# Joining f64 weights in a PSUM bank, reordering the first attention tiles, and splitting w_out one block later

## The chip, the cores and the metric

The kernel runs on one core of a Trainium2 chip. The metric is the device time of one execution in microseconds (us), the median of several runs. The engines are TensorE (PE; its weight loads are PEld), VectorE (DVE), ScalarE (ACT), GpSimd (POOL) and SyncE (SP), which here only issues transfers. Each works through its own queue in program order and waits on semaphores for the others.

## The reference

```
k_p, v_p = k, v averaged over groups of 8 positions      # 8 batches, 8 heads, 576 -> 72
attn = softmax(q @ k_p.T / 8) @ v_p                       # + 1e-9 in the denominator
x = attn as 4608 tokens x 512
h = x @ w_in                                              # 512 -> 2048, w_in and w_out arrive as f64
g = where(h >= 1, h, where(h <= -1, 0, (h + 1)**2 / 4))
y = g @ w_out                                             # 2048 -> 512
e = argmax(y @ w_gate) of 8 experts, p = its softmax weight
out = p * (max(y @ w1[e], 0) @ w2[e])
```

## The kernel before

The 4608 tokens are 36 tiles of 128 rows, in ten blocks of 3, 4 x 7, 3 and 2 tiles. The routed experts follow and are not touched by the change.

**A block of the feed-forward** runs over m = 0 to 15, the 128-wide slices of the hidden dimension. `f1(j, m)` forms h for the slice with 12 matmuls in ps0 or ps1; `f2(j, m)` adds the slice's part of y with 9 or 12 matmuls into ps2 and up. f1 runs two steps (`AHEAD`) ahead of f2. Each operand is split into a high part and a remainder (hi, lo), so a product takes three matmuls (L593 to L595, L621 to L623). Behind f1's matmuls come L600 (VectorE, clamp), L601 (ScalarE, square), then, put off through the list `later`, `larger`: L605 (VectorE, maximum) and L606 (ScalarE, high part of g), and at the next flush `lower`: L264 on VectorE (remainder of g), which frees ps0 or ps1. `slot(j, s)` is called twice per step, s = 2m and 2m + 1, here called the even and the odd half of a step. It calls `tick` (block 0 only), then one or two of the attention units of the next block's tiles, then `flush`, which runs what stands in `later`; in block 0 also one pooling step of the next batch's K and V.

**Converting the weights.** w_in and w_out are f64; slices are loaded as pairs of 32-bit words into six buffers RB, and 32 conversions (`order`) make f32 of them in block 0 and before it:
- a, `convert_a`: ScalarE copies the scaled high word into the target (L527; WOF for w_out, DFI for w_in, three or four buffers each) and the sign into SGN (L531);
- b, `convert_b`: two VectorE operations, the "pair": L539 joins low word and sign into CV, which is the PSUM bank ps5, and L542 shifts the target and joins CV into it. They are put on the list `pend` and issued by `mix()`, at the latest by the next tick's `mix(4)`;
- c, `convert_c`: ScalarE casts the high part (L549), POOL subtracts (`low_part`, L264), and for w_out SP stores both parts, 512 KB, to wo_d (L552).

`tick` number n does mix(4), the load of a later slice, c(n - 2), a(n) and b(n). Eight ticks are issued around the first two f1; in block 0's loop there is one in each half-step for m = 0 to 11, one in each of steps 12 and 13, and none after that. Conversions count from 0. From block 1 on `load_out` brings both parts of w_out back, 512 KB a step, on the ScalarE queue.

**Attention of a tile t** is cut into units: q transposed (TensorE; L368 copies), scores (TensorE L312; VectorE L319, L321 twice each; then exp, ScalarE L326, and the row sum L376, L378, L379), the probabilities turned (first three tiles: TensorE L412 and ScalarE L414, two copies; tiles 3 to 6: VectorE transposes L396, L398, and an exchange through DRAM, p_d, on SP's queue), and the product with V (TensorE L425; ScalarE L431 high part of x, VectorE L432 low part). The division is on POOL (L382, L390). Before block 0, K and V of batch 0 are pooled: K heads 0 to 3 on TensorE (`u_kp`), the others on VectorE (L249, one reduction) or POOL (L252 to L254), and tiles 0 to 2 are done with their units interleaved.

The order on each engine is the order in which these functions are called; nothing is reordered.

Of the kernel before, what the change touches and what calls it, by code (L numbers as in the profile page):

```python
# [8 lines left out]
F32 = mybir.dt.float32  # L9
# [15 lines left out]
def attention_ffn_routed_experts_kernel(  # L25
# [47 lines left out]
    wo_d = dram.tile([KF, 128, 2, DM], F32R, name="wo_d")  # L73
    yrow_d = dram.tile([NT + 128, ROW], F32, name="yrow_d")
# [35 lines left out]
    KB = [at(576 * i, 4 * SP_).rearrange("p (a c) -> p a c", a=4) for i in range(2)]  # L110
    QB = [at(1152 + 512 * i, 512) for i in range(2)]
    QB2 = at(6336, 512)
    QT = at(2176, 512)
    SC = [at(2688, 576), at(7616, 576)]
    HEAD = blocks[0][1]
    RAW = [at(3264 + 512 * i, 512, SP_) for i in range(3)]
# [7 lines left out]
    PZ = at(1152, 768).rearrange("p (a h j) -> p a h j", a=3, j=32)  # L124
# [162 lines left out]

    def u_kt_pair(b, c):

        pb = bank()  # L290
        nc.tensor.transpose(pb[:, 0:SP_], KP[:, c * 128:(c + 1) * 128], ident[0:SP_, 0:SP_])
        nc.scalar.activation(out=KB[b][:, c], in_=pb[:, 0:SP_], func=ACTF.Copy)

# [10 lines left out]
    def u_sc_all(t):  # L304
# [10 lines left out]
        sc, sc3, smx = sc_of(t), sc3_of(t), smx3[:, t % 3]  # L315
# [9 lines left out]
        def exps():  # L325
            nc.scalar.activation(out=sc, in_=sc, func=ACTF.Exp, scale=1.0 / 64)  # L326
            finish(t)
        if HEAD <= t < TURN0:
# [7 lines left out]
    SCH = at(6848, 576)  # L336
    PTX = [WOF[2][0:SP_], WOF[3][0:SP_], PT[:, 0], PT[:, 1]]
# [7 lines left out]
    def sc3_of(t):  # L345
        return sc_of(t).rearrange("p (h c) -> p h c", h=H)

    def pt_of(t, hf):
        return PTX[(2 * t + hf) % 4] if t < HEAD else PT[:, hf]
# [22 lines left out]
    def finish(t):  # L372
        sc3, ssm = sc3_of(t), ssm3[:, t % 3]

        def rest():
            nc.vector.tensor_reduce(out=ssm, in_=sc3, axis=AX.X, op=ALU.add)  # L376
            mix()
            nc.vector.tensor_scalar(ssm, ssm, 1e-9, None, op0=ALU.add)  # L378
# [144 lines left out]
    def convert_a(i):  # L523
        dst, rb = cvt_dst(i)

        high = rb[:, :, :, 1].bitcast(F32)
        nc.scalar.activation(out=dst.rearrange("p (a x) -> p a x", a=8), in_=high,  # L527
# [5 lines left out]
    def convert_b(i):  # L533
# [6 lines left out]
            out=ci, in0=rb[:, :, :, 0], scalar=29, in1=sg, op0=ALU.logical_shift_right,  # L540
            op1=ALU.bitwise_or))
        pend.append(lambda: nc.vector.scalar_tensor_tensor(  # L542
            out=di, in0=di, scalar=3, in1=ci, op0=ALU.logical_shift_left, op1=ALU.bitwise_or))

    def convert_c(i):
# [5 lines left out]
        if o:  # L551
            nc.sync.dma_start(out=r32(wo_d[m]), in_=r32(WO[:, m % 4]))  # L552
# [19 lines left out]
    def tick():  # L572
# [5 lines left out]
        for f, i in ((convert_c, n - 2), (convert_a, n), (convert_b, n)):  # L578
            if 0 <= i < len(order) and order[i]:
                f(i)  # L580
# [876 lines left out]
```

## Time and profile before

| what | value |
|---|---|
| median of 3 runs (lowest, highest) | 1401.77 us (1400.38, 1402.29) |
| the profiled execution's own time | 1404.79 us |
| its span, first to last instruction | 1402.8 us |
| granted TensorE clock, mean over the span | 0.993 |
| busy PE / DVE / ACT / POOL | 1357.5 / 778.1 / 433.7 / 358.7 us |
| busy in the first 38.10 us, PE / DVE / ACT / POOL | 23.60 / 22.32 / 18.67 / 19.50 us |
| one L326 / L431 on ScalarE | 0.69 / 0.58 us |
| one L601, 384 wide, on ScalarE | 0.62 us |
| one L379 on VectorE | 0.20 us |

The profile is one execution. A duration is given from the start of the work to its end, and on VectorE and ScalarE the next instruction often starts a little before the end of the one ahead. A busy TensorE is not one at its full rate. A note in square brackets on a timeline row is the engine's idle time before the instruction, and what ended it.

### The profile page before, as it was taken

The numbers are of one execution on the slowest core, as the hardware profiler recorded it, in microseconds if no ns is written. First come the engines' busy times: TensorE is split into PE (matmuls) and PEld (weight loads), VectorE is DVE, ScalarE is ACT, GpSimd is POOL, SyncE is SP. The second block draws the span as 40 slices with busy tenths as digits, with TensorE's granted clock in tenths as the row PEclk, the third lists the DMA queues.
The fourth block names the chain that finished last, engine by engine and source line by source line (L and its number), as shares of the span: only waits on it lengthen the run. The fifth ranks groups of instructions, "written<-read, shape, count | busy, mean of one in ns | idle before, by whom it ended". The sixth has DMA issues, their size and how long they took to land. (4 is left out here: it accounts for less than half of the span.)

```text
span 1402.8 us, 22101 instructions
## 1 busy us (share of the span) xinstructions
PE 1357.5 (97%) x8082; PEld 1112.8 (79%) x8082; DVE 778.1 (55%) x1577; ACT 433.7 (31%) x729; POOL 358.7 (26%) x520
## 2 busy tenths in 40 slices
PE   6878999999999999999999999999999999999998
PEld 4767778878878778788788888888878888888786
DVE  5798556565666666575666556455532333323426
ACT  4567332222222222223222223343111111111335
POOL 5384736004304203413310011022221211111212
PEclk9999999999999999999999999999999999999999
DMA  9786647436636555545553344572543223331235
GB/s 254 226 261 240 182 136 214 129 122 194 164 124 187 153 149 168 171 155 143 165 157 111 98 152 130 192 263 72 195 129 106 91 74 113 99 111 61 79 127 187
DMA packets 170701, 213.45 MB, mean 152 GB/s; under 512 B 83432, under 2 KB 114440, under 8 KB 170569
## 3 DMA queue, kind: packets, MB, share of 16 engines
q1 hardware_dynamic: 135992, 102.29, 25.2%
q10 hardware_dynamic: 26784, 88.16, 18.8%
q0 software_dynamic: 7792, 21.35, 4.8%
q8 instruction: 69, 1.13, 0.3%
q14 instruction: 64, 0.52, 0.1%
HBM read 188.30 MB, written 47.03 MB: 168 GB/s over the span
## 5 line engine op out<-in xcount | busy, mean ns | idle before, releaser
L593 PE MATMUL ps<-XT,W 128*128 128x512 f32 (+2 forms) x640 | 243.8, 381 | 6.8 <-DVE FG L264 3.0
L595 PE MATMUL ps<-XT,W 128*128 128x512 f32 (+2 forms) x640 | 237.9, 372 | 2.7 <-POOL W L264 2.7
L594 PE MATMUL ps<-XT,W 128*128 128x512 f32 (+2 forms) x640 | 238.1, 372 | 0.2 <-DVE XT L432 0.2
L621 PE MATMUL ps<-WO,FG 128*128 128x512 f32 x576 | 231.6, 402 | 1.3 <-ACT FX L601 1.1
L622 PE MATMUL ps<-WO,FG 128*128 128x512 f32 x576 | 225.9, 392 | 0.0
L623 PE MATMUL ps<-WO,FG 128*128 128x512 f32 x576 | 225.2, 391 | 0.0
L601 ACT ACTIVATE FX<-FX,half 128x512 f32<-128x512 f32 (+2 forms) x152 | 104.0, 684 | 386.0 <-DVE FX L600 348.2
L600 DVE TENSOR_SCALAR FX<-ps 128x512 f32<-128x512 f32 (+2 forms) x152 | 96.7, 636 | 117.7 <-PE ps L595 116.9
L593 PEld LDWEIGHTS ps<-XT,W 128*128 128x128 f32 x640 | 121.8, 190 | 32.1 <-issue 3.4
L719 POOL DMA_INDIRECT perm_d<-idt,POSI x36 | 35.2, 978 | 417.6 <-DVE SM L705 353.0
L993 DVE SCALAR_TENSOR_TENSOR FG<-ps,FG 128x512 fp32r<-128x512 f32 (+1 forms) x64 | 43.2, 675 | 175.4 <-ACT FG L992 172.9
L595 PEld LDWEIGHTS ps<-XT,W 128*128 128x128 f32 x640 | 121.7, 190 | 22.3 <-POOL W L264 4.0
L605 DVE TENSOR_TENSOR ps<-FX,ps 128x512 f32<-128x512 f32 (+2 forms) x152 | 97.5, 641 | 72.8 <-ACT FX L601 71.4
L594 PEld LDWEIGHTS ps<-XT,W 128*128 128x128 f32 x640 | 121.7, 190 | 17.8 <-DVE XT L432 0.5
L621 PEld LDWEIGHTS ps<-WO,FG 128*128 128x128 f32 x576 | 108.5, 188 | 26.4 <-issue 3.0
L623 PEld LDWEIGHTS ps<-WO,FG 128*128 128x128 f32 x576 | 108.6, 188 | 23.7
L606 ACT ACTIVATE FG<-ps 128x512 fp32r<-128x512 f32 (+2 forms) x160 | 88.8, 555 | 123.9 <-DVE ps L605 112.2
L264 DVE TENSOR_TENSOR FG<-ps,FG 128x512 fp32r<-128x512 f32 (+2 forms) x160 | 100.8, 630 | 44.3 <-ACT FG L606 40.6
L622 PEld LDWEIGHTS ps<-WO,FG 128*128 128x128 f32 x576 | 108.7, 189 | 19.8
L252 POOL TENSOR_TENSOR AT<-AT 72x256 f32<-72x256 f32 x106 | 81.2, 766 | 136.3 <-DMA AT<-in_v_dram 68.7
L992 ACT ACTIVATE FG<-ps 128x512 fp32r<-128x512 f32 (+1 forms) x64 | 37.4, 584 | 244.8 <-PE ps L989 231.2
L987 PE MATMUL ps<-XT,W 128*128 128x512 f32 (+1 forms) x256 | 98.9, 386 | 2.9 <-ACT XT L971 2.5
(230 smaller groups left out, 2176.0 us busy)
## 6 DMA issues: line engine op xcount, KB each, us to landing
WO<-wo_d ACTq DMA_DIRECT2D x144, 512.0 KB
AT<-in_moe_w_dram SPq DMA_DIRECT2D x30, 1024.0 KB
p_d<-AT SPq DMA_DIRECT2D x29, 384.0 KB
AT<-in_v_dram SPq DMA_DIRECT2D x59, 144.0 KB
wo_d<-WO SPq DMA_DIRECT2D x16, 512.0 KB
AT<-in_k_dram SPq DMA_DIRECT2D x56, 144.0 KB
PT<-p_d SPq DMA_DIRECT2D x58, 128.0 KB
yrow_d<-Y ACTq DMA_DIRECT2D x7, 1032.0 KB
```

Source lines behind the costliest of these rows:

```text
L264: eng.tensor_tensor(out=lo, in0=x, in1=r32(hi), op=ALU.subtract)
L593: nc.tensor.matmul(o, wi(m, 0, c), xh, start=(c == 0), stop=False)
L594: nc.tensor.matmul(o, wi(m, 0, c), xl, start=False, stop=False)
L595: nc.tensor.matmul(o, wi(m, 1, c), xh, start=False, stop=(c == KD - 1))
L600: nc.vector.tensor_scalar(r, o, -1.0, 1.0, op0=ALU.max, op1=ALU.min)
L601: nc.scalar.activation(out=r, in_=r, func=ACTF.Square, scale=0.5, bias=half)
L605: nc.vector.tensor_tensor(out=o, in0=r, in1=o, op=ALU.max)
L606: nc.scalar.activation(out=gh, in_=o, func=ACTF.Copy)
L621: nc.tensor.matmul(o, gh, WO[:, g % 4, 0], start=(m == 0), stop=False)
L622: nc.tensor.matmul(o, gh, WO[:, g % 4, 1], start=False, stop=False)
L623: nc.tensor.matmul(o, gl, WO[:, g % 4, 0], start=False, stop=(m == KF - 1))
L987: nc.tensor.matmul(o, e1(0)[:, c, ms], xh, start=(c == 0), stop=False)
```

## The change

- Conversion: a's first copy goes into CV instead of the target; the pair then shifts CV and joins the sign (one PSUM input), and joins the low word to that into the target (one PSUM input). `tick` puts a and b of conversion n into `later`, so they follow `larger` or `lower` in the flush; all pending pairs are issued first.
- w_out: c still makes both parts for block 0's own use, but SP stores the joined f32, 256 KB, to a new tensor wf_d. From step 11 of block 0 on, `split_out` loads it back two slices ahead; for block 1 ScalarE and POOL split it again, and SP stores both parts, 512 KB, to wo_d, from which blocks 2 and later load as before.
- Row sums: the scores get a 73rd column that holds 1e-9, so L378 goes.
- First tiles: V heads 8 to 11 are pooled on TensorE (`u_vp`), K head 6 on VectorE; the loads of V are reordered; six buffers hold turned probabilities; the units of tiles 0, 1, 2 are called one tile after the other, exp and row sums in an order written out; q of tile 2 is transposed ahead of the scores of tile 1. Four ticks instead of six come before the first f1, four instead of two behind it and the second. Several buffers move within AT and VS.

```diff
     wo_d = dram.tile([KF, 128, 2, DM], F32R, name="wo_d")
+    wf_d = dram.tile([KF, 128, DM], F32, name="wf_d")
     yrow_d = dram.tile([NT + 128, ROW], F32, name="yrow_d")
...
+    def u_vp(more):
+
+        pb = bank()
+        n = len(RAW)
+        raw = at(RAW0, n * 512, SP_).rearrange("p (h r d) -> p h r d", h=n, r=8)
+        for x, h0, h1 in ((raw, 0, n), (more.rearrange("p (h r d) -> p h r d", h=1, r=8), n, n + 1)):
+            dst = pb[0:SP_, h0 * D:h1 * D].rearrange("p (h d) -> p h d", h=h1 - h0)
+            for r in range(8):
+                nc.tensor.matmul(dst, ident[0:SP_, 0:SP_], x[:, :, r], start=(r == 0),
+                                 stop=(r == 7))
+        nc.scalar.activation(out=VS[:, 0, 0:(n + 1) * D], in_=pb[0:SP_, 0:(n + 1) * D],
+                             func=ACTF.Copy)
+
     def u_kt_pair(b, c):
...
                                      kb[rows, c], start=True, stop=True)
-        sc, sc3, smx = sc_of(t), sc3_of(t), smx3[:, t % 3]
+        sc3, smx = sc3_of(t), smx3[:, t % 3]
         for i in range(2):
...
         def exps():
-            nc.scalar.activation(out=sc, in_=sc, func=ACTF.Exp, scale=1.0 / 64)
+            nc.scalar.activation(out=sc3, in_=sc3, func=ACTF.Exp, scale=1.0 / 64)
             finish(t)
-        if HEAD <= t < TURN0:
+        if t < TURN0:
             later.append(exps)
...
-    SCH = at(6848, 576)
-    PTX = [WOF[2][0:SP_], WOF[3][0:SP_], PT[:, 0], PT[:, 1]]
+    SCH = at(6848, SCW)
+    PTX = [VS[:, 1], FR[0:SP_], PT[:, 0], PT[:, 1], WOF[2][0:SP_], WOF[3][0:SP_]]
...
+    def sc4_of(t):
+        return sc_of(t).rearrange("p (h c) -> p h c", h=H)
+
     def sc3_of(t):
-        return sc_of(t).rearrange("p (h c) -> p h c", h=H)
+        return sc4_of(t)[:, :, 0:SP_]
     def pt_of(t, hf):
-        return PTX[(2 * t + hf) % 4] if t < HEAD else PT[:, hf]
+        return PTX[2 * t + hf] if t < HEAD else PT[:, hf]
...
         def rest():
-            nc.vector.tensor_reduce(out=ssm, in_=sc3, axis=AX.X, op=ALU.add)
-            mix()
-            nc.vector.tensor_scalar(ssm, ssm, 1e-9, None, op0=ALU.add)
+            nc.vector.tensor_reduce(out=ssm, in_=sc4_of(t), axis=AX.X, op=ALU.add)
+            if t >= HEAD:
+                mix()
             nc.vector.reciprocal(out=ssm, in_=ssm)
...
     def convert_a(i):
-        dst, rb = cvt_dst(i)
+        _, rb = cvt_dst(i)
         high = rb[:, :, :, 1].bitcast(F32)
-        nc.scalar.activation(out=dst.rearrange("p (a x) -> p a x", a=8), in_=high,
+        nc.scalar.activation(out=CV.rearrange("p (a x) -> p a x", a=8), in_=high,
                              func=ACTF.Copy, scale=2.0 ** -112)
...
         pend.append(lambda: nc.vector.scalar_tensor_tensor(
-            out=ci, in0=rb[:, :, :, 0], scalar=29, in1=sg, op0=ALU.logical_shift_right,
+            out=ci, in0=ci, scalar=3, in1=sg, op0=ALU.logical_shift_left, op1=ALU.bitwise_or))
+        pend.append(lambda: nc.vector.scalar_tensor_tensor(
+            out=di, in0=rb[:, :, :, 0], scalar=29, in1=ci, op0=ALU.logical_shift_right,
             op1=ALU.bitwise_or))
-        pend.append(lambda: nc.vector.scalar_tensor_tensor(
-            out=di, in0=di, scalar=3, in1=ci, op0=ALU.logical_shift_left, op1=ALU.bitwise_or))
+
+    def convert_ab(i):
+        mix(len(pend))
+        convert_a(i)
+        convert_b(i)
...
         if o:
-            nc.sync.dma_start(out=r32(wo_d[m]), in_=r32(WO[:, m % 4]))
+            nc.sync.dma_start(out=wf_d[m], in_=dst)
...
             more_raw(n - 1 + NRB)
-        for f, i in ((convert_c, n - 2), (convert_a, n), (convert_b, n)):
-            if 0 <= i < len(order) and order[i]:
-                f(i)
+        if 0 <= n - 2 < len(order) and n != 3:
+            convert_c(n - 2)
+        if n < len(order):
+            later.append(lambda: convert_ab(n))
         ticks[0] += 1
...
         nc.scalar.dma_start(out=r32(WO[:, g % 4]), in_=r32(wo_d[g % KF]))
+
+    def split_out(g):
+
+        if g < 2 * KF - 2:
+            nc.scalar.dma_start(out=WOF[(g + 2) % 4], in_=wf_d[(g + 2) % KF])
+        if g >= KF:
+            hi, lo = WO[:, g % 4, 0], WO[:, g % 4, 1]
+            nc.scalar.activation(out=hi, in_=WOF[g % 4], func=ACTF.Copy)
+            low_part(lo, WOF[g % 4], hi)
+            nc.sync.dma_start(out=r32(wo_d[g % KF]), in_=r32(WO[:, g % 4]))
...
             nc.scalar.activation(out=gh, in_=o, func=ACTF.Copy)
-            if KF <= g + 1 < len(steps):
+            if KF <= g + 3 <= 2 * KF + 1:
+                split_out(g + 1)
+            elif 2 * KF < g + 2 <= len(steps):
                 load_out(g + 1)
...
         wgp = WG.rearrange("p e d -> p (e d)")[0:SP_]
-        raw0 = [WG[0:SP_, i] for i in range(8)] + RAW + [
+        raw0 = [WG[0:SP_, i] for i in range(6)] + [VS[:, 1], PT[:, 1]] + RAW + [
             FX[0:SP_, 512 * i:512 * (i + 1)] for i in range(1, 5)] + [PT[:, 0]]
...
+        nc.gpsimd.memset(WG[:, 6:8], 0.0)
+        for t in range(3):
+            nc.gpsimd.memset(sc4_of(t)[:, :, SP_:SP_ + 1], 1e-9)
         load_q(0)
...
         load_q(2)
-        for i in range(H, 2 * H):
+        for i in (12, 13, 8, 9, 10, 11, 14, 15):
             load_kv(0, i, raw0[i])
...
             u_kp(0, c, wgp[:, 1024 * c:1024 * (c + 1)])
-        for i in (4, 5):
+        for i in (4, 5, 6):
             head_pool(i, nc.vector)
-        for i in (6, 7):
-            head_pool(i, nc.gpsimd)
-        nc.gpsimd.memset(WG[:, 6:8], 0.0)
+        head_pool(7, nc.gpsimd)
         for i in range(3, NRB):
...
             u_kt_pair(0, c)
-        for i in (8, 10, 12):
+        for i in (12, 13, 14):
             head_pool(i, nc.gpsimd)
         hu[0][2]()
+        hu[2][0]()
+        later.popleft()()
         hu[1][2]()
-        hu[2][0]()
-        head_pool(9, nc.vector)
-        head_pool(14, nc.gpsimd)
+        rest = later.popleft()
+        later.popleft()()
+        rest()
+        head_pool(15, nc.gpsimd)
+        later.popleft()()
+        hu[2][2]()
+        exps2 = later.popleft()
+        tick()
         flush()
-        hu[2][2]()
-        head_pool(15, nc.gpsimd)
-        for i in (11, 13):
-            head_pool(i, nc.vector)
+        u_vp(raw0[11])
+        exps2()
         load_pair(0)
         load_pair(1)
+        hu[0][3]()
+        flush()
+        hu[0][5]()
+        hu[0][6]()
+        tick()
+        flush()
+        hu[1][3]()
+        hu[1][5]()
+        hu[1][6]()
+        tick()
+        hu[2][3]()
+        hu[2][5]()
+        convert_c(1)
+        hu[2][6]()
         flush()
         tick()
+        flush()
         kv = deque([pair_step(c) for c in range(4)] + [kv_step(1, i) for i in range(H, 2 * H)])
-        line = [(0, 3), (0, 5), (1, 3), (0, 6), (1, 5), (2, 3), (1, 6), (2, 5), (2, 6)]
-        for i, (t, n) in enumerate(line):
-            hu[t][n]()
-            flush()
-            if i in (0, 2, 4, 6):
-                tick()
-        while ticks[0] < CAHEAD + 1:
-            tick()
         banks.clear()
...
             flush()
-            tick()
+            while ticks[0] < CAHEAD + 2 + m:
+                tick()
+                flush()
         for g, (j, m) in enumerate(steps):
```

## Rows read from the trace of the kernel before

**Rows 1.** Windows, block 1: us; busy PE, PEld, DVE, ACT, POOL; clock; DMA share; GB/s.
```profile
146.70:240.00 93.30, 92.87 (x593) 74.25 (x594) 58.29 (x119) 28.62 (x48) 48.73 (x99) 1.00 0.64 180
```

**Rows 2.** Source views of four lines: ns minimum/median/maximum, first to last start us.
```profile
L539 DVE SCALAR_TENSOR_TENSOR ps<-Y,WG x12: 684/702/2096, 26.2 to 141.5; 128x512 int32<-128x512 int32 x12
...
L542 DVE SCALAR_TENSOR_TENSOR FX<-FX,ps x32: 673/687/690, 26.9 to 142.3; 128x512 int32<-128x512 int32 x32
...
L378 DVE TENSOR_SCALAR ssm<-ssm x36: 171/173/1276, 19.5 to 854.2; 128x8 f32<-128x8 f32 x36
...
L264 POOL TENSOR_TENSOR WO<-FX,WO x16: 1258/1284/1471, 45.2 to 148.5; 128x512 fp32r<-128x512 f32 x16
```

**Rows 3.** Windows, conversions 8 to 30: VectorE alone, then line 539 alone.
```profile
50.61:134.92 84.31, 73.44 (x118) 0.92 0.82 265
...
50.61:134.92 84.31, 23.28 (x22) 0.92 0.82 265
```

**Rows 4.** Timeline of VectorE in block 0: start us, us, instruction [idle before].
```profile
43.55 0.56 DVE L605 TENSOR_TENSOR ps<-FX,ps 128x384 f32<-128x384 f32 x1 [0.69 <-ACT FX L601]
44.02 0.69 DVE L539 SCALAR_TENSOR_TENSOR ps<-WG 128x512 int32<-128x512 int32 x1
44.75 0.69 DVE L542 SCALAR_TENSOR_TENSOR FX<-FX,ps 128x512 int32<-128x512 int32 x1
45.35 0.55 DVE L600 TENSOR_SCALAR AT<-ps 128x384 f32<-128x384 f32 x1
```

**Rows 5.** Timeline of ScalarE: head, one step, conversions 8 and 30.
```profile
27.41 0.59 ACT L414 ACTIVATE PT<-ps 72x512 f32<-72x512 f32 x1
...
44.15 0.49 ACT L606 ACTIVATE FG<-ps 128x384 fp32r<-128x384 f32 x1 [0.63 <-DVE ps L605]
44.53 0.62 ACT L549 ACTIVATE WO<-FX 128x512 fp32r<-128x512 f32 x1
45.05 0.66 ACT L527 ACTIVATE FX<-Y 128x512 f32<-128x512 f32 x1
45.60 0.78 ACT L531 ACTIVATE WG<-Y 128x512 f16<-128x512 f32 x1
...
50.61 0.67 ACT L527 ACTIVATE FX<-AT 128x512 f32<-128x512 f32 x1
...
134.92 0.66 ACT L527 ACTIVATE FX<-Y 128x512 f32<-128x512 f32 x1
```

**Rows 6.** Timeline of VectorE: attention work.
```profile
14.38 0.46 DVE L319 TENSOR_REDUCE smx<-ps 128x4 f32<-128x288 f32 x1 [4.27 <-PE ps L312]
...
16.10 0.45 DVE L319 TENSOR_REDUCE smx<-ps 128x4 f32<-128x288 f32 x1
...
25.11 0.73 DVE L376 TENSOR_REDUCE ssm<-AT 128x8 f32<-128x576 f32 x1
...
30.22 0.69 DVE L432 SCALAR_TENSOR_TENSOR XT<-ps,XT 128x512 fp32r<-128x512 f32 x1 [1.04 <-ACT XT L431]
...
92.43 0.70 DVE L396 STREAM_TRANSPOSE AT<-AT 128x512 f32<-128x512 f32 x1
...
93.39 0.42 DVE L319 TENSOR_REDUCE smx<-ps 128x4 f32<-128x288 f32 x1
```

**Rows 7.** Timeline of TensorE: value product, f1, block 1's first matmul.
```profile
30.48 1.98 PE L425 MATMUL ps<-PT,VS 72*64 72x128 f32 x16
...
38.11 0.69 PE L593 MATMUL ps<-XT,W 128*128 128x384 f32 x1 [1.42 <-DVE XT L432]
...
42.11 0.34 PE L593 MATMUL ps<-XT,W 128*128 128x384 f32 x1
...
146.73 0.50 PE L593 MATMUL ps<-XT,W 128*128 128x512 f32 x1 [0.48 <-ACT XT L431]
```

**Rows 8.** Timeline of POOL in the head.
```profile
9.47 0.72 POOL L252 TENSOR_TENSOR WG<-WG 72x256 f32<-72x256 f32 x1 [8.02 <-DMA WG<-in_k_dram]
...
12.78 0.95 POOL L1138 MEMSET WG<- 128x1024 f32 x1
```

More of the change, by code (lines that the diff above doesn't have):

```diff
@@ L108, in fx @@
         return FX[:, o:o + n]
-    KB = [at(576 * i, 4 * SP_).rearrange("p (a c) -> p a c", a=4) for i in range(2)]
-    QB = [at(1152 + 512 * i, 512) for i in range(2)]
+    KB = [at(288 * i, 4 * SP_).rearrange("p (a c) -> p a c", a=4) for i in range(2)]
+    QB = [at(1160 + 512 * i, 512) for i in range(2)]
     QB2 = at(6336, 512)
-    QT = at(2176, 512)
-    SC = [at(2688, 576), at(7616, 576)]
+    QT = at(7616, 512)
+    SCW = H * (SP_ + 1)
+    SC = [at(2184, SCW), at(576, SCW)]
     HEAD = blocks[0][1]
-    RAW = [at(3264 + 512 * i, 512, SP_) for i in range(3)]
+    RAW0 = 3264
+    RAW = [at(RAW0 + 512 * i, 512, SP_) for i in range(3)]
     KP = at(4800, 512, SP_)
@@ L123, in attention_ffn_routed_experts_kernel @@
     JK = at(7104, 512)
-    PZ = at(1152, 768).rearrange("p (a h j) -> p a h j", a=3, j=32)
+    PZ = at(1160, 768).rearrange("p (a h j) -> p a h j", a=3, j=32)
     PZ0 = at(6336, 768).rearrange("p (a h j) -> p a h j", a=3, j=32)
```

## The prediction

> **What bounds the kernel now.** First the windows [rows 1]. In block 1 TensorE is busy 92.87 of 93.30 us, and the later blocks are built like it, so time is made or lost before about 147 us: in the head (to 38.1 us) and in block 0, which converts the f64 weights while it computes. There the window that I use runs from the start of conversion 8 (50.61) to that of conversion 30 (134.92) [rows 5]: 84.3 us for 11 steps of m, 7.7 us a step. VectorE is busy 73.4 us of it [rows 3]; a step's matmuls need less. So VectorE's queue sets the pace of block 0, not TensorE.
>
> Next, what fills that queue. In the views by line [rows 2], L539 (both inputs in SBUF) takes 0.68 to 2.1 us for the same work, while L542 (one input in PSUM) never takes more than 0.69. In the window 22 of L539 take 23.28 us [rows 3]: 23.28 - 22 x 0.69 = 8.1 us of stalls. L378 ranges from 0.17 to 1.28 us in the same way.
>
> Last the timelines, for the hand-overs. With the starts in [rows 4, 5]: L605 to the next VectorE start 0.47; the pair L539, L542 takes 0.73 + 0.69 = 1.42 (0.08 of it overlaps what follows); L605's end to L606's start 0.04; L606 to the next ScalarE start 0.38 (the other way I take 0.04 as well); L527 0.55, then L531 0.78, so 1.33 for the two; the cast L549 0.52 to the next start, and so the square, which is as wide. A step without attention work is then 4.7 us: L600 0.47; pair 1.34; meanwhile ScalarE does the square 0.52, the cast 0.52 and the two of the next conversion 1.33, so the second pair starts at 0.47 + 0.04 + 2.37 + 0.04 = 2.9 and its successor at 4.25; L264 0.47. What matters: **before, ScalarE's two run while VectorE is still joining the conversion ahead** (L527 at 45.05, L542 at 44.75), as each conversion has its own target.
>
> Check of the method: 11 x 4.7 = 51.7; attention work on VectorE, four tiles: scores 4 x 1.72 (14.38 to 16.10), transposes 4 x 0.96 (92.43 to 93.39), three low parts of x at 0.61, four row sums at 0.87 without L378 and about 1.2 for L378 [rows 2, 6]: 20.8; stalls 8.1. Sum 80.6 of 84.3; 3.7 is left for waits.
>
> **The change, part by part.**
> *Joining in PSUM.* Both new VectorE operations have one PSUM input, like L542, so I take 0.69 for each: the 8.1 us go, and L378 goes (4 x 1.2 = 4.8 us). Bounds: L542's 0.69 and L539's 2.1. Gross, 12.9 us less VectorE work in the window.
>
> But the high word is now written by ScalarE into CV, which is one bank, and stays there until the second operation of the pair has read it. The next conversion's first write must wait for that. The steps become a ring. Even half: the pair ends; L605 (behind it in VectorE's queue) 0.47; hand-over 0.04; L606 0.38 (in ScalarE's queue ahead of the conversion, which is now put behind the flush); the two 1.33; hand-over 0.04; next pair 1.42: 3.68. Odd half: 0.04 + 1.33 + 0.04 + 1.42 = 2.83. Together **6.5 us a step, against 4.7**. The copy into PSUM is taken at L527's 0.55; nothing in the trace writes PSUM from ScalarE.
>
> The Trainium skill (PSUM — Partial Sum Buffer, section on bank collisions) says that two engines may not touch one bank in the same partitions at once, whichever addresses they use. By that rule a second half-bank buffer would not loosen the ring either; if overlap as before were possible, the step would stay at 4.7. The trace of before has no ScalarE write to CV, so it cannot show it.
>
> Attention work that sits in the ring adds to it. 32 units are dealt over 27 half-steps. In even halves they stand ahead of L605: two row sums 1.7, three pairs of transposes 2.9, three sets of scores 5.2, three low parts 1.8: 11.6 us. In odd halves VectorE has 1.4 us free while ScalarE works, of which L264 and L600 take 0.94: two sets of scores exceed by 1.24 each, one pair of transposes 0.5, two row sums 0.4 each: 3.8. So the window becomes 11 x 6.5 + 15.4 = **86.9 us against 84.3**: the stalls saved are given back by the ring. Bounds: 82 (the odd ones hidden, ScalarE's write 0.1 cheaper), 91 (the 3.7 of other waits stays too).
>
> *The head.* On POOL two K heads were pooled one after the other, 9.47 to 12.78, 1.65 each [rows 8]. One goes to VectorE, so the last is ready up to 1.65 earlier; TensorE's own work ahead of it leaves 0.7: first scores at 13.7 instead of 14.38 [rows 6]. Then VectorE in its new order: scores 0 1.7, scores 1 (behind tile 2's q transposes on TensorE, 15.85) 1.75, two row sums 1.75 with their exp hand-over, scores 2 1.75: 21.1. Exp 0.7, two copies 0.5 each (L414, [rows 5]; 0.59 long, 0.1 of it overlapped), so tile 0's value product starts at 23.0. The V product on TensorE in place of pooling lies beside this. Now each tile is finished before the next: product 2.0 [rows 7], ScalarE's high part 0.55, low part 0.7 [rows 6], the last join of conversion 0 0.7, conversion 1's two 1.35, two copies 1.0: tile 1 starts at 29.3. Product 2.0, high part 0.6, cast 0.5, two copies 1.1: tile 2 at 33.5. Product, high and low part 3.4: first f1 matmul at **36.9 against 38.11**: 1.2 us gained. Bounds: 34 and 38.
>
> But only conversion 2's two and, behind its pair, conversion 3's come before it (before: those of 4 and, nearly, 5). The rest falls into the ring. The first f1 takes 4.0 us (38.11 to 42.11, [rows 7]), to 40.9; L600, square and L605 to 42.7; conversion 3's pair ends at 44.1 and conversion 4 starts. Then 46.9, 49.7; conversion 7 after L600, the square and L605 of the second f1, 53.6; pair of 7 ends 56.4; L605 and L606, so **conversion 8 starts at 57.3 against 50.61: 6.7 us late**. Bounds: 52 (TensorE at its faster spacing in the head) to 59.
>
> *Sum.* Conversion 30 at 57.3 + 86.9 = 144.2 against 134.92: +9.3. Behind it: its pair to 147.0; L264 and a row sum, L600 at 148.3, pair of 31 to 150.2, L605, L606, L264 to 151.7, L600 and tile 6's low part to 152.9: block 1's first matmul at 152.9 against 146.73 [rows 7]. In the last three steps, where conversions run out, 3.1 us come back. **+6.2 us.**
>
> *w_out stored joined.* Block 0 stores 16 x 256 KB instead of 512: 4.2 MB less of the window's 265 GB/s; a store waits for VectorE and no longer for POOL, so SP's loads behind it go earlier. VectorE's ring, not a transfer, sets block 0: 0. Bounds 0 to -3.7 (the other waits). Block 1 gets 16 casts (0.62, 9.9 us of ScalarE, 28.6 of 93.3 busy) and 16 subtractions (1.28 each, 20.6 us of POOL, 48.7 of 93.3 busy) [rows 1, 2, 5], loads of 256 KB instead of 512, and 16 stores of 512 KB on SP, ahead of K, V and q loads and attention's exchange. Each is issued about three steps before its product, f1 runs two steps ahead, DMA is at a share of 0.64: cost 0, hidden under TensorE. If that cover went, one late subtraction would hold a product by 0.62 + 1.28; for the first two, 4. Later blocks load w_out as before.
>
> The profiled execution took 1404.79 (span 1402.8, 2.0 around it), 3.0 above the median 1401.77. The sum is a difference and is put on the median: 1401.8 + 6.2 = **1408.0**.
>
> **Rivals.**
> *Faster: the ring does not close.* If ScalarE's next copy overlaps the join as before, VectorE stays the bound and its stalls are a plain gain: 84.3 - 12.9 = 71.4. Two more conversions fall behind the first f1, at 2.35 each, less the 1.2 gained: +3.5. Net -9.4: 1392.4. For it: VectorE's 73.4 of 84.3. Against: one bank, and the flush order. It decides when the ring costs under 5 us a step.
> *No change.* TensorE already at its faster spacing in the head (f1's matmuls are 0.34 long from 42.11 on, up to 0.69 before, [rows 7]): three products 1.0 shorter, the first f1 1.9: 6.2 - 4.9 = +1.3, 1403. Against: before, with TensorE busier, it stayed slow until 42.
> *The joins still wait for POOL* (the change does not do what it says): the 8.1 stays, inside the ring: 1416. Against: L542's 690 ns maximum over 32. Or TensorE, now with gaps of 2 us a step, falls back to 1.2 GHz (granted 0.92 in the window, [rows 3]): 2 us a time, four times, also 1416.
>
> **How the numbers follow.** My case 0.60 (own range 1403 to 1414, by the bounds), faster 0.18, no change 0.12, worse 0.10. A measurement of this kernel tells 0.2% (2.8 us) from no change. The edge of my case lies near it: 0.02 of it counts as faster and 0.03 as the same; 0.02 of no change as slower. Faster 0.20, same 0.13, slower 0.67. The range 1391 to 1418 takes in the faster case and most of the worse one.
>
> **What would show it.** Right: first f1 near 37; both joins at 0.69, L378 gone; ScalarE's L527 idle before it, ended by VectorE's second join; conversion 8 near 57 and 30 near 144; VectorE under 70% busy between; block 1 still 99% TensorE with POOL near 69. Wrong: L527 running during the join ahead, or VectorE still near 87% there; a first f1 before 34; gaps on TensorE in block 1.

## The result and the profile after

The changed kernel takes 1418.56 us (median of 4, 1416.78 to 1423.90) against 1402.03 before (median of 4 runs by then), a ratio of 1.0127 (95% interval 1.0098 to 1.0155): 16.5 us slower. Forecast were 1408.0, between 1391 and 1418, and slower. So the sign is right, the size is 2.7 times the one worked out, and the time lies 0.6 us outside the range. The profiled execution took 1423.90, 5.3 over the median; its span is 1422.1.

First the steps by their time marks, on TensorE the first f1 matmul of blocks 0 and 1, on ScalarE the first copies of conversions 8 and 30 (timelines of the changed kernel; start us, us, instruction):

```profile
35.02 0.69 PE L628 MATMUL ps<-XT,W 128*128 128x384 f32 x1 [0.70 <-ACT XT L450]
...
161.69 0.39 PE L628 MATMUL ps<-XT,W 128*128 128x512 f32 x1
```
```profile
55.61 0.62 ACT L546 ACTIVATE ps<-AT 128x512 f32<-128x512 f32 x1
...
148.47 0.62 ACT L546 ACTIVATE ps<-Y 128x512 f32<-128x512 f32 x1 [0.38 <-POOL AT L257]
```

Against [rows 5, 7], with the forecast in brackets: the first f1 is 3.1 us earlier (1.2), conversion 8 is 5.0 late (6.7), conversion 30 13.6 late (9.3), block 1's first f1 15.0 late (6.2). Between conversions 8 and 30 lie 92.86 us (86.9). Then the windows of conversions 8 to 30 and of block 1 (columns as in [rows 1]):

```profile
55.61:148.47 92.86, 74.59 (x589) 62.72 (x590) 63.01 (x116) 57.03 (x104) 45.91 (x53) 0.87 0.69 205
161.70:255.00 93.30, 89.93 (x569) 71.97 (x568) 55.72 (x108) 32.90 (x57) 57.62 (x98) 0.96 0.65 192
```

VectorE's work fell from 73.44 [rows 3] to 63.01, as wanted, and the window got longer all the same. In block 1, TensorE is idle for 3.4 us, where it was for 0.4 [rows 1], and its granted clock is 0.96, where it was 1.00. The group of VectorE's first join in the first of these windows (operation, shapes, count | busy us, mean ns | idle before it and what ended it):

```profile
L558 DVE SCALAR_TENSOR_TENSOR ps<-ps,WG 128x512 int32<-128x512 int32 x22 | 15.3, 697 | 22.1 <-ACT WG L550 22.1
```

A mean of 697 ns: the stalls of L539 [rows 2] are gone. But before this operation VectorE stands idle for 22.1 us, which it did not for L539 in the same stretch of the kernel before (the largest of its three groups there; the other two have 0.0):

```profile
L539 DVE SCALAR_TENSOR_TENSOR ps<-WG 128x512 int32<-128x512 int32 x12 | 12.3, 1024 | 0.3
```

The waits of the changed kernel in its window (total us, times, longest), and one step in the timeline of VectorE and ScalarE:

```profile
DVE ps L558 <- ACT WG L550: 22.1, 16, 1.8
...
ACT FG L641 <- DVE ps L640: 18.5, 12, 3.7
...
ACT ps L546 <- DVE FX L560: 9.8, 11, 1.0
```
```profile
128.11 0.65 ACT L546 ACTIVATE ps<-Y 128x512 f32<-128x512 f32 x1 [0.44 <-DVE FX L560]
...
131.17 0.56 DVE L640 TENSOR_TENSOR ps<-AT,ps 128x384 f32<-128x384 f32 x1
131.76 0.49 ACT L641 ACTIVATE FG<-ps 128x384 fp32r<-128x384 f32 x1 [0.24 <-DVE ps L640]
132.15 0.62 ACT L546 ACTIVATE ps<-AT 128x512 f32<-128x512 f32 x1
132.69 0.76 ACT L550 ACTIVATE WG<-AT 128x512 f16<-128x512 f32 x1
...
133.49 0.70 DVE L558 SCALAR_TENSOR_TENSOR ps<-ps,WG 128x512 int32<-128x512 int32 x1 [1.76 <-ACT WG L550]
```

Two loops are to be seen here. One is the ring that was forecast: ScalarE's copy into the bank waits for the second join (L560), 11 times. The other is longer and would be there without the bank: VectorE's larger part L640, ScalarE's cast L641, both copies, and only then VectorE's join. The copies stand behind L641 because the change queues a conversion behind the flush. Which of the two sets the time the profile alone does not tell.

### The profile page after: what moved, and what is told of

Same layout as the page of the kernel before. It is cut to its first block, busy times and chain, and to the rows that moved or that the text cites. A ratio compares the mean times of both kernels' runs of the same rounds, so it can differ in the third digit from the quotient of the medians.

```text
span 1422.1 us, 22172 instructions
## 1 busy us (share of the span) xinstructions
PE 1369.4 (96%) x8114; PEld 1123.4 (79%) x8114; DVE 759.0 (53%) x1539; ACT 443.9 (31%) x746; POOL 371.9 (26%) x533
## 5 line engine op out<-in xcount | busy, mean ns | idle before, releaser
L628 PEld LDWEIGHTS ps<-XT,W 128*128 128x128 f32 x640 | 122.8, 192 | 37.1 <-ACT W L573 10.9
L640 DVE TENSOR_TENSOR ps<-FX,ps 128x512 f32<-128x512 f32 (+2 forms) x152 | 97.5, 642 | 72.6 <-ACT FX L636 72.6
L641 ACT ACTIVATE FG<-ps 128x512 fp32r<-128x512 f32 (+2 forms) x160 | 88.9, 556 | 133.8 <-DVE ps L640 126.3
L267 DVE TENSOR_TENSOR FG<-ps,FG 128x512 fp32r<-128x512 f32 (+2 forms) x160 | 100.8, 630 | 44.1 <-ACT FG L641 42.8
L255 POOL TENSOR_TENSOR AT<-AT 72x256 f32<-72x256 f32 x104 | 76.5, 735 | 104.1 <-DMA AT<-in_v_dram 60.5
```

Of the source, the lines that this page charges most:

```text
L267: eng.tensor_tensor(out=lo, in0=x, in1=r32(hi), op=ALU.subtract)
L628: nc.tensor.matmul(o, wi(m, 0, c), xh, start=(c == 0), stop=False)
L640: nc.vector.tensor_tensor(out=o, in0=r, in1=o, op=ALU.max)
L641: nc.scalar.activation(out=gh, in_=o, func=ACTF.Copy)
```

## The theories

**Ring theory** (that of the prediction): the one PSUM bank makes a loop of ScalarE and VectorE. **Deferral theory**: the loss comes from the place of the two copies behind the flush, whatever the join's buffer. **Sign theory**, a part of both: the sign copy, which the first join waits for, is the second of the two. **Order theory** (in the expectations of the first runs): the conversions are called late, and TensorE stops at 50 to 65 us. **Split theories**: the later split of w_out, costed at nothing, is not hidden, because of its stores or because of its cast and subtraction. In each experiment a ratio is to the kernel before, run on the same chip beside it.

Two marks per run are used below: the start of the sign copy of conversions 8 and 30 (it exists in every version), and the first f1 of block 1.

## Experiments 1 to 4: taking parts away

**Old joins** (`e1_old_joins`): the high word goes to SBUF again; all else as changed.

```
-  out=CV.rearrange(...), in_=high             # ScalarE
+  out=dst.rearrange(...), in_=high
-  out=ci, in0=ci, scalar=3, in1=sg            # VectorE, first join
-  out=di, in0=rb[:, :, :, 0], scalar=29, in1=ci
+  out=ci, in0=rb[:, :, :, 0], scalar=29, in1=sg
+  out=di, in0=di, scalar=3, in1=ci
```

> The changed kernel with the joins of before (high word copied to the conversion's own target, L539-like and L542-like pair), all else as changed. Ring theory (ScalarE's write to the one PSUM bank waits for VectorE's second join, and that sets block 0): the two ScalarE operations run during the pair ahead again, the stretch from conversion 8 to 30 falls from 92.9 us to about 80 (84.3 before, less 4.8 for the removed row-sum addition), VectorE stalls on POOL return (about 8 us); time 1403 to 1408. Order theory (the loss is conversions called late plus TensorE's gap at 50 to 65 us): the stretch keeps its 11 us hole behind conversion 9, time 1413 or more.

1415.83, ratio 1.0086 (1.0070 to 1.0103): only 2.7 less than the changed kernel. The ring theory's number is missed, and the window stays at 92.91 us, where it forecast about 80. The time lies in the order theory's range.

**w_out as before** (`e2_both_parts`): block 0 stores two parts, block 1 loads them.

```
-  nc.sync.dma_start(out=wf_d[m], in_=dst)
+  nc.sync.dma_start(out=r32(wo_d[m]), in_=r32(WO[:, m % 4]))
-  if KF <= g + 3 <= 2 * KF + 1:
-      split_out(g + 1)
-  elif 2 * KF < g + 2 <= len(steps):
+  if KF <= g + 1 < len(steps):
       load_out(g + 1)
```

> The changed kernel with w_out stored and loaded as before (both parts, 512 KB, from block 0; no splitting in block 1). Ring theory: block 0 is not set by stores, so the start of block 1 stays at 161 to 162 us; in block 1 the 7.5 us wait of VectorE for q goes back to 2.6 and TensorE's 3.4 us gap with it; time 1413 to 1418. Storing theory (the later split makes SP's queue late and that is the main loss): time 1408 or less.

1412.08, ratio 1.0072 (1.0055 to 1.0089): the split costs 6.5 here. The time lies in neither range, and block 1 starts at 155.73, not at 161 to 162 as the ring theory has it.

**Order only** (`e3_order_only`): both edits together. The head's order, the place behind the flush and the padded row sum are left.

> The changed kernel with the joins of before and w_out stored as before: what is left is the order of the first tiles, the late ticks and the padded row sum. Ring theory: 1399 to 1404, since the first f1 comes 3 us earlier and L378 is gone, against conversions called later. Order theory: still 1410 or more.

1406.33, ratio 1.0029 (1.0015 to 1.0042): again between the two ranges. VectorE's waits between conversions 8 and 30 of this run:

```profile
DVE ps L558 <- ACT WG L550: 19.8, 11, 1.8
```

Here the copy goes to SBUF and never waits for a join, so there is no ring, and VectorE still waits 1.8 us, 11 times; with the joins in PSUM (`e2_both_parts`) it is 22.2 us in 17 times, so the bank adds some 2.4 us. The window has 92.46 us here and 92.11 there. So the ring does not set it. What the ring does set is the stretch without attention work: conversions 4, 5 and 6 begin 2.83 and 2.84 us apart in the changed kernel and 1.71 apart in this one, and conversion 8 begins at 54.46 with joins in PSUM, at 48.23 without (1.9 of these 6.2 us stand at the first f1 already, 32.91 against 31.06). The medians put the joins at 5.8.

**Sign copy first** (`e4_sign_first`):

```
+  nc.scalar.activation(out=sign[:, :, :, 1], in_=high, ...)
   nc.scalar.activation(out=CV.rearrange(...), in_=high, ...)
-  nc.scalar.activation(out=sign[:, :, :, 1], in_=high, ...)
```

> The changed kernel with ScalarE's two operations exchanged: the sign, which has two buffers, is written first, then the high word into the PSUM bank. Ring theory: in the odd halves only the 0.6 us copy is left in the ring (2.8 to 2.1 us), in the even halves nothing changes: 11 x 0.7 = 8 us shorter between conversions 8 and 30, some 2 more around the first f1; time 1407 to 1411. If the bank is not what ScalarE waits for: no change, 1416 to 1420.

1412.90, ratio 1.0067 (1.0050 to 1.0084): 5.7 less than the changed kernel, and above the ring theory's range. The sign copy writes no PSUM, so it may run while the bank is still being read; only the other copy is in the ring then. The window is 89.44, 3.4 shorter and not 8, and VectorE still waits 19.1 us, now for the copy into PSUM.

## Experiments 5 to 8: the place of the copies, and the stores

**Sign first and ahead of the flush** (`e5_sign_first_in_tick`):

```
   if n < len(order):
-      later.append(lambda: convert_ab(n))
+      convert_ab(n)
```

> The changed kernel with two edits: ScalarE makes the sign copy before the copy into PSUM, and a conversion's copies stand in the queues ahead of the flush (as in the kernel before), not behind it. Deferral theory: what slows block 0 is that each conversion's two copies are queued on ScalarE behind the cast of the larger part, so that VectorE waits 1.8 us for the sign copy in every even half whatever buffer is used (10 waits with PSUM joins and 10 with the old joins). Then VectorE's waits for the sign copy in the window of conversions 8 to 30 fall from about 20 us to under 8, the window from 92.9 to 84 to 88, and the time from 1418.6 to 1408 to 1412 (the later split of w_out, some 6.5 to 9.5, is left). Ring theory (the one PSUM bank alone sets the pace): the copy into PSUM still waits for the second join, the window stays at 89 or more, as with the sign first alone, and the time at 1412 to 1414.

1404.92, ratio 1.0019 (1.0008 to 1.0029): 8.0 less than with the sign first alone and 13.6 less than the changed kernel, more than the deferral theory asked for. The window is 79.10 us, shorter than before the change (84.30), and the wait is nearly gone (waits of VectorE between conversions 8 and 30; the sign first shifts lines by one):

```profile
DVE ps L557 <- ACT ps L548: 3.2, 10, 0.4
```

The edit also puts the pair on VectorE's list that much earlier; no run moves the one without the other.

**The same with w_out as before** (`e6_tick_both_parts`):

> The run before this one, with w_out stored as two parts in block 0 and read as two parts in block 1, as before the change. What is left of the change is the order of the head, the joins in PSUM (sign first) and the padded row sum. Deferral theory: 1398 to 1404. Ring theory: 1405 to 1409 (order plus part of the ring). If the later split of w_out costs 6.5 to 9.5 whatever stands beside it, this run lies that much under the one before it.

1402.86, ratio 1.0000 (0.9988 to 1.0012), in the deferral theory's range. The split costs 2.1 here, not 6.5 to 9.5.

**Old joins, ahead of the flush** (`e7_old_joins_in_tick`), that is `e3_order_only` with the edit of one line above:

> The order alone once more (joins of before, w_out as before), but with the conversions queued ahead of the flush as before: the new head, its earlier first f1 and the padded row sum are what is left. Deferral theory: the window of conversions 8 to 30 goes from 92.5 back to 83 to 87, and the time from 1406.3 to 1396 to 1402. Rival (the order costs because fewer conversions are done before block 0 starts, not because of where they are queued): 1404 to 1408, as without the edit.

1400.21, ratio 0.9976 (0.9965 to 0.9987): faster than before the change. The edit took 6.1 us where ScalarE copies nothing into the bank, and the window went from 92.46 to 83.86; both lie in the deferral theory's ranges. VectorE's wait for the sign copy in this window, 19.8 us in `e3_order_only`, is now:

```profile
DVE ps L558 <- ACT WG L550: 3.0, 9, 0.5
```

VectorE's first joins in that window of both runs, `e3_order_only` and then this one (window, length, busy us and count, clock, DMA share, GB/s):

```profile
48.23:140.69 92.46, 17.67 (x22) 0.89 0.76 240
```
```profile
51.85:135.71 83.86, 22.12 (x22) 0.86 0.81 265
```

Where VectorE waits for ScalarE anyhow, the join stalls little (17.67, against 22 x 0.69 = 15.2 unstalled); where the wait is gone the stalls come back (22.12, before 23.28, [rows 3]). So the two costs hide each other in part: 16.8 us of waits went and 4.5 us of stalls came. Why there are fewer stalls beside the waits was not shown. Removing the stalls alone bought nothing (`e10_before_psum` below).

**Block 1's stores issued by GpSimd** (`e8_store_on_pool`):

```
-  nc.sync.dma_start(out=r32(wo_d[g % KF]), in_=r32(WO[:, g % 4]))
+  nc.gpsimd.dma_start(out=r32(wo_d[g % KF]), in_=r32(WO[:, g % 4]))
```

> The changed kernel with one edit: block 1's stores of the two parts of w_out are issued by GpSimd, which makes the subtraction, and no longer by SyncE. Queue theory: the loads of Q and V heads stand behind these stores in SyncE's queue, and each store waits for GpSimd's subtraction, so the loads come late (a wait of 7.5 us for a Q load in block 1) and TensorE stops; then the wait goes, block 1 loses no time between its steps 5 and 7, and the time is 4 to 7 us less, 1412 to 1415. Traffic theory (16 loads of 256 KB and 16 stores of 512 KB more compete with the Q and V loads, or ScalarE and GpSimd are late): 1416 to 1420, the wait stays.

1424.30, ratio 1.0150 (1.0119 to 1.0181): slower still by 5.7, outside both ranges. First what it was to cure. In the changed kernel SyncE's queue (start, us, issues), and the VectorE transpose of a Q tile that waits for a load from it, after and then before the change:

```profile
186.47 3.66 SPq L230 DMA_DIRECT2D AT<-in_q_dram  x4
190.24 0.40 SPq L620 DMA_DIRECT2D wo_d<-WO  x1
190.74 0.34 SPq L246 DMA_DIRECT2D AT<-in_v_dram  x1
191.13 2.28 SPq L230 DMA_DIRECT2D AT<-in_q_dram  x4
```
```profile
195.04 0.71 DVE L377 STREAM_TRANSPOSE AT<-AT 128x512 f32<-128x512 f32 x1 [7.46 <-DMA AT<-in_q_dram]
...
176.26 0.71 DVE L358 STREAM_TRANSPOSE AT<-AT 128x512 f32<-128x512 f32 x1 [2.56 <-DMA AT<-in_q_dram]
```

VectorE's queue stands behind this wait, and TensorE behind VectorE; then TensorE's clock falls to 0.50 (1.2 GHz) for 6.8 us (TensorE's wait, then a window):

```profile
199.98 1.51 PE L694 MATMUL ps<-WG 128*32 128x96 f32 x32 [3.37 <-DVE WG L686]
```
```profile
199.00:205.80 6.80, 5.82 (x42) 4.64 (x43) 2.88 (x5) 2.27 (x5) 3.72 (x7) 0.50 0.66 178
```

From the first f1 of block 1 to that of its step 7 the changed kernel takes 48.6 us, before 43.5: 5.1 lost here, 3.4 of them by the stop; the rest goes with the clock, at which f1's matmuls start 0.43 us apart and not 0.23. With the stores on GpSimd these steps take 44.7 and the wait is 5.32, but later another load is late, that of P for a value product (VectorE's wait, then TensorE's):

```profile
190.16 0.71 DVE L377 STREAM_TRANSPOSE AT<-AT 128x512 f32<-128x512 f32 x1 [5.32 <-DMA AT<-in_q_dram]
```
```profile
232.90 1.97 PE L444 MATMUL ps<-PT,VS 72*64 72x128 f32 x16 [2.48 <-DMA PT<-p_d]
```

From step 11 to 12 it takes 12.3 us where the kernel before takes 6.7. So it seems that the queue's order decides which load is late, and that one is late at all comes from the traffic or the split itself.

## Experiments 9 to 12: telling the rest apart

**Ahead of the flush alone** (`e11_in_tick`), the sign copy second as changed:

> The changed kernel with one edit alone: a conversion's two copies stand in ScalarE's queue ahead of the flush, not behind it; the order of the two copies stays as changed. Deferral theory: most of what the two edits together gave (13.7 us) is this one: window of conversions 8 to 30 at 80 to 87, time 1404 to 1410. Rival (the edits share the gain evenly, because the bank's ring is half of it): 1411 to 1414, window 87 to 90.

1412.39, ratio 1.0069 (1.0054 to 1.0085): 6.2 less. The window is 83.20, in the deferral theory's range, but the time is in the rival's: conversion 8 begins at 57.18, where with the sign first too it begins at 52.19 (1.6 of this stand at the first f1, 36.43 against 34.81). Its waits between conversions 8 and 30:

```profile
DVE ps L558 <- ACT WG L550: 7.0, 13, 0.9
ACT ps L546 <- DVE FX L560: 6.8, 17, 0.6
```

So the deferral is not "most of it": the two edits take 6.2 and 5.7 alone and 13.6 together. The deferral acts in the window, the sign copy in the head as well.

**The split without its stores** (`e9_split_no_store`): `e5_sign_first_in_tick`, with the parts stored by block 0 beside the joined words, and not by block 1.

```
 # convert_c
   nc.sync.dma_start(out=wf_d[m], in_=dst)
+  nc.sync.dma_start(out=r32(wo_d[m]), in_=r32(WO[:, m % 4]))
 # split_out
-  nc.sync.dma_start(out=r32(wo_d[g % KF]), in_=r32(WO[:, g % 4]))
```

> The changed kernel with the sign first, conversions ahead of the flush, and a change in where w_out's parts are stored: block 0 stores the joined words and the two parts, block 1 splits the joined words but stores nothing. So the later split is left with its loads, casts and subtractions and without its stores. Store theory (16 stores of 512 KB ahead of and beside the Q and V loads make a Q load late): the wait of VectorE's Q transpose falls from 7.8 to under 4 us and block 1 loses under 1.5 us between its steps 5 and 7, where it lost 5.6; block 0 gets up to 3 us longer by its added stores; 1401 to 1405. Split theory (the cast and subtraction, or the loads, are late): the 5.6 us stay, 1406 to 1409.

1406.98, ratio 1.0031 (1.0021 to 1.0041). This lies in the split theory's range. But block 0 stores three times as much here and ends 4.6 us later, and the time is lost where no edit reaches: at the first f1 of block 2 this run is 1.6 us ahead of `e5_sign_first_in_tick` (245.98 against 247.61), and in its profiled execution the routed experts' matmuls and what follows take 3.3 us longer (450.2 against 446.9). Block 1 by itself tells: the first f1, that of step 7 and the Q wait, in `e5_sign_first_in_tick` and then in this run:

```profile
142.65 0.39 PE L627 MATMUL ps<-XT,W 128*128 128x512 f32 x1
...
191.78 0.50 PE L627 MATMUL ps<-XT,W 128*128 128x512 f32 x1
```
```profile
176.85 0.71 DVE L377 STREAM_TRANSPOSE AT<-AT 128x512 f32<-128x512 f32 x1 [7.83 <-DMA AT<-in_q_dram]
```
```profile
147.29 0.40 PE L627 MATMUL ps<-XT,W 128*128 128x512 f32 x1
...
190.13 0.50 PE L627 MATMUL ps<-XT,W 128*128 128x512 f32 x1
```
```profile
177.45 0.71 DVE L377 STREAM_TRANSPOSE AT<-AT 128x512 f32<-128x512 f32 x1 [3.85 <-DMA AT<-in_q_dram]
```

49.1 us with the stores, 42.8 without (before 43.5), with all the loads, casts and subtractions of the split still there. So block 1's loss comes from the 16 stores of 512 KB. Whether by their place in the queue or by their traffic was not separated: issued by GpSimd they made another load late.

**Joins in PSUM alone** (`e10_before_psum`): the kernel before with the joins of `e6_tick_both_parts`.

> The kernel before with one part of the change alone: the joins in PSUM, the sign copy first. Head order, place of the conversions ahead of the flush, row sum and w_out are those of before. If joins in PSUM are a gain where ScalarE's copies are not queued behind the flush: the window of conversions 8 to 30 falls from 84.3 to 78 to 82 as in the two runs with them, and the time to 1396 to 1400 (faster). Rival (the ring costs in the head what the window gives, as the run with joins in PSUM was 2.7 us slower than that with the old joins): 1401 to 1405.

1404.37, ratio 1.0015 (1.0006 to 1.0024). A miss: the gain that the window of the two runs with these joins seemed to promise is not there. Its window is 87.13, not 78 to 82, and conversion 8 begins at 53.52, 2.3 late (the first f1 2.8 late already, at 40.92). The time lies in the rival's range. It agrees with the pair `e7_old_joins_in_tick` and `e6_tick_both_parts`, where the same joins cost 2.7.

**The sign first with old joins** (`e12_old_joins_sign_first`): `e7_old_joins_in_tick` with the edit of experiment 4.

> The fastest so far (new head order, padded row sum, old joins, w_out stored as before, conversions ahead of the flush; 1400.2), with one edit: ScalarE makes the sign copy before the high copy. The first of the old joins reads only the sign copy, so it may start one copy (0.65) sooner. If VectorE's wait for the sign copy is still on the path: 1397 to 1399.5. If not (in that run's window this wait is no longer among the ten largest): 1399.5 to 1402.

1399.79, ratio 0.9984 (0.9971 to 0.9996): not to be told from `e7_old_joins_in_tick`, as expected if the wait is off the path: with those joins and that place, the sign copy is not seen on it. These two are the fastest versions, 2.3 to 2.7 us under the kernel before.

## Why the prediction was wrong in size

A chain of runs that differ by one edit each, in its first two steps by two, adds up to the whole change:

| from, to | edit | median us | step |
|---|---|---|---|
| before to `e7_old_joins_in_tick` | new head, padded row sum | 1402.5 to 1400.2 | -2.3 |
| to `e6_tick_both_parts` | joins in PSUM, sign first | 1402.9 | +2.7 |
| to `e5_sign_first_in_tick` | w_out joined, split later | 1404.9 | +2.1 |
| to `e4_sign_first` | copies behind the flush | 1412.9 | +8.0 |
| to the changed kernel | sign copy second | 1418.6 | +5.7 |

The steps depend on what stands beside them: the place behind the flush costs 6.1 to 8.0, the sign copy second 5.7 to 7.5, the split 2.1 to 9.5, the joins in PSUM 2.1 to 5.8. The intervals of the ratios are 1.3 to 4 us to either side, so a step of 2 or 3 us is not certain by itself.

**Right.** Both joins at 0.69 and VectorE under 70% busy in the window (63.01 of 92.86). The ring in size: 2.83 us for an odd half was worked out and 2.83 and 2.84 are measured (conversions 4 to 6); 3.9 and 3.7 were worked out from conversion 6 to 7 and from 7 to 8 (49.7, 53.6, 57.3), and 3.76 and 3.73 are measured. The sign of the change, and that the stalls saved buy nothing. From conversion 10 to 30, ten steps of 6.5 with 14 of attention (ten elevenths of the 15.4) make 79.0; the sign copies of the changed kernel are 79.05 apart there.

**Right in size, wrong in name.** The even half's 3.68 was put down to the bank, "the stalls saved are given back by the ring". It is the way through the flush, L640 and L641 and then both copies, and `e3_order_only` has it with no copy into the bank: its copies of conversions 6, 7 and 8 start 3.77 and 3.75 apart, and from conversion 10 to 30 it takes 78.6. So the agreement of the 79.0 does not speak for the ring. The prediction saw that the conversion "is now put behind the flush" and priced it, but took it for a part of the ring. That is why the first experiment missed.

The rule of the Trainium skill (PSUM — Partial Sum Buffer, the section on bank collisions) could not be tested: CV is both one bank and one buffer, so the same addresses are in question too. The trace shows the wait, 9.8 us in 11 times, and not whether a second half of the bank would have ended it.

**The step that failed most: w_out "stored joined" at "cost 0, hidden under TensorE".** It costs 6.5 us from `e2_both_parts` to the changed kernel, and 5.1 are seen in block 1. Looked at were the cast and the subtraction, which do hide, and the DMA share of 0.64; the 16 stores of 512 KB "ahead of K, V and q loads" were named, and no wait for those loads was priced. What the runs show in its place: in block 1's first seven steps the five runs with these stores on SyncE's queue lose 3.0 to 5.6 us against the kernel before, the seven without these stores between -0.7 and 0.7. Of the credit allowed in block 0, "0 to -3.7", 3.2 can be seen in one pair: block 1's first f1 is at 145.81 in `e6_tick_both_parts` and at 142.65 in `e5_sign_first_in_tick`, and 1.0 of it stands at the first f1 of block 0 (35.85 and 34.81). In the other pairs it cannot. In `e1_old_joins` the first f1 of block 1 is 4.0 later than in `e3_order_only`, and 2.3 of that stand there already at the first f1 of block 0, before any store of w_out; this part of the 9.5 stays open. So does a last one: from the first matmul of the routed experts to the end, the profiled executions of the seven runs with the joined w_out take 446.9 to 450.7 us, those of the seven without 444.2 to 446.9, though no edit reaches there.

**The window: 86.9 forecast, 92.86 measured.** The excess of 6 is one step, conversions 8 to 10, which takes 13.8 us (sign copies) and was counted at the mean 7.9. It took 10.9 before the change already, so a mean over steps was the wrong term. TensorE stands still there for a Q copy that ScalarE makes late, and VectorE then for f1 (timelines of the changed kernel):

```profile
54.09 0.58 ACT L387 ACTIVATE AT<-ps 128x512 f32<-128x512 f32 x1
54.72 0.34 PE L328 MATMUL ps<-AT 64*64 64x72 f32 x2 [4.12 <-ACT AT L387]
...
65.68 0.56 DVE L635 TENSOR_SCALAR AT<-ps 128x384 f32<-128x384 f32 x1 [5.10 <-PE ps L630]
```
```profile
55.00:65.00 10.00, 6.97 (x74) 6.55 (x74) 3.72 (x8) 4.53 (x9) 1.81 (x2) 0.53 0.89 246
```

The last row is a window: behind TensorE's stop the granted clock is 0.53 from 55 to 65 us, and f1's matmuls start 0.32 us apart, where they were 0.17 apart at 44 us. `e7_old_joins_in_tick` has the wait too (4.0) and takes 12.7 for this step; `e10_before_psum`, with the joins in PSUM and the old head, takes 10.9 like the kernel before. So most of the hole belongs to the new head, not to the joins.

**The end of block 0.** 3.1 us were to come back after conversion 30; 1.4 were lost. That is of this execution: `e8_store_on_pool` has the same block 0 (its stores begin behind it), and there 1.7 do come back (9.6 us from the sign copy of conversion 30 to block 1's first f1, 12.7 in the changed kernel, 11.2 before the change). In both TensorE waits 2.9 us for a remainder of g ahead of its last f1; from there to block 1's first f1 the same 38 matmuls get another clock (windows of the changed kernel, then of `e8_store_on_pool`):

```profile
151.86:161.69 9.83, 9.83 (x38) 8.25 (x39) 5.74 (x11) 5.71 (x11) 8.88 (x14) 0.51 0.37 99
```
```profile
151.27:158.05 6.78, 6.78 (x38) 5.98 (x38) 4.41 (x9) 4.50 (x9) 5.98 (x10) 0.79 0.44 121
```

In `e8_store_on_pool` block 1 starts 11.3 late, and together with the changed kernel's 5.1 in block 1 that would make 16.4, near the 16.5 of the medians.

**The rivals.** "Faster: the ring does not close" came true in the window alone once the copies stood ahead of the flush, 79.10 us and not 71.4. Block 1 then starts 4.1 us before that of the kernel before (142.65 against 146.73), and the stores take back 5.6 in its first seven steps. "No change" rested on TensorE at its faster spacing in the head; in the profiled execution of `e3_order_only` it had it (granted clock 1.00 to 45 us), and the first f1 came at 31.06. "The joins still wait for POOL" is refuted by the mean of 697 ns. TensorE at 1.2 GHz came true in part: the clock fell behind TensorE's stops at 50 us, in block 1 and at the end of block 0, where it cost 3 us in this execution. It does not set the window of conversions 8 to 30: the clock was 0.86 in the 83.86 us of `e7_old_joins_in_tick` and 0.89 in the 92.46 us of `e3_order_only`. The 1416 of these two rivals lies nearer to the measured time than the forecast, but by luck: the one is refuted, and four losses of 2 us by the clock are not what adds up here. POOL in block 1 was expected near 69 us and has 57.62: the 14 subtractions in that window take 18.0, as priced, and its other work there 39.6, before 47.4.

## What to carry to other kernels

Before a buffer is blamed for a loop, look at what stands ahead of the loop's first instruction in its engine's queue: here, moving two copies ahead of a flush was worth 6 to 8 us, and giving the copy that the reader waits for the first place another 5.7 to 7.5, as long as that reader did wait. Stalls inside an instruction and waits ahead of it can hide each other, so stalls saved count only where the engine is not made to wait instead. A store that "only moves" to a later stage is priced by the loads that come behind it, by what waits for the latest of them, and not by the mean share of the DMA engines (0.65 here).

## What was not expected of the hardware

TensorE's granted clock in the head differs between executions of the same code. The changed kernel and `e8_store_on_pool` are the same up to block 1. In the profiled execution of the one the clock has fallen to 0.50 (1.2 GHz) before 25 us; in that of the other it is at 1.00 (2.4 GHz) until then, and TensorE gets through 49 matmuls from 20 to 25 us where the first has 26 (windows of the changed kernel, then of `e8_store_on_pool`):

```profile
20.00:25.00 5.00, 3.70 (x26) 2.83 (x27) 2.36 (x5) 3.24 (x7) 4.62 (x6) 0.65 1.09 391
25.00:30.00 5.00, 3.03 (x22) 2.44 (x22) 1.98 (x3) 2.67 (x5) 0.00 (x0) 0.50 0.98 166
```
```profile
20.00:25.00 5.00, 4.08 (x49) 3.42 (x47) 3.26 (x8) 3.69 (x7) 4.13 (x6) 1.00 1.08 385
25.00:30.00 5.00, 2.18 (x19) 1.74 (x18) 1.80 (x3) 2.27 (x5) 0.00 (x0) 0.79 0.99 198
```

From 10 to 20 us TensorE had been busy for 8.91 us in the first. What made the difference the rows do not show, so a start that differs by 1 or 2 us between two profiles is no effect of an edit by itself.

The same 128x512 copy on ScalarE takes 0.62 to 0.66 us into PSUM (changed kernel), 0.65 to 0.71 into SBUF (`e3_order_only`).
